# Moving the mask setup, eight gathers, a q load and the token weights' layout, and giving small attention operations to ScalarE, in a fused block-sparse attention and mixture-of-experts kernel

## The chip, the cores and the metric

The kernel runs on one core of a Trainium2 chip. The metric is the device time of one execution in microseconds (us). The core has five instruction streams that run in order and wait for one another through semaphores: TensorE (PE, whose weight loads are listed apart as PEld), VectorE (DVE), ScalarE (ACT), GpSimd (POOL) and SyncE (SP), which here only issues transfers.

## The reference

The program computes a block-sparse attention and feeds it to a small mixture of experts. There are 4 batches, 8 heads, 768 positions and 64 elements per head. Positions form 24 blocks of 32. A block of queries sees its own block and its two neighbours, the first and the last block, and three sampled blocks; the first and the last block of queries see everything.

```python
scores = scale * np.matmul(q, k.transpose(0, 1, 3, 2))
mask = np.abs(blk_i - blk_j) <= 1
mask = mask | (blk_i == 0) | (blk_j == 0) | (blk_i == n_blocks - 1) | (blk_j == n_blocks - 1)
for qb in range(n_blocks):
    for kb in sampled_blocks[qb]:
        mask[qb*32:(qb+1)*32, kb*32:(kb+1)*32] = True
attn = softmax(where(mask, scores, -1e9))      # sum + 1e-9 in the denominator
x = (attn @ v) as 3072 tokens x 512
p = domain_probs / (domain_probs.sum(-1) + 1e-9)
for e in range(4):
    out += p[:, e:e+1] * (relu(x @ w1[e]) @ w2[e])   # 512 -> 1024 -> 512
```

## The kernel before, in words

**Two kinds of attention units.** A batch has 16 units. Four are "Edge" units: for the first and the last query block, all heads at once against one half of the keys (`m` = 0 or 1); the two halves are joined afterwards with the running maximum (`mx`), the weight `w` and the sums. Twelve are "Group" units: four neighbouring query blocks `t` with four heads (`u` = 0 or 1) against 8 slots of keys. Each unit has four steps: `S` (scores into PSUM, maxima, exponentials), `T` (transposes of the probabilities through PSUM into `pt`), `A` (product with v, reciprocal of the sums, scaling into `xg`) and `X` (transpose of the result into `xr`, the expert layers' input). A Group's `S` ends in four rounds of one DVE operation (mask, add, minimum, L372) and one ACT exponential (L374). The reciprocal in `A` starts from `sums + 1e-9` (L402); for an Edge from `sums0 * w + 1e-9 + sums1` (L481, L482).

**Batch 0, the setup.** For batch 0 the units run as a software pipeline, loop L1164: in round `n` the program writes `S` of unit `n`, `X` of `n-3`, `A` of `n-2` and `T` of `n-1`. POOL and ACT copy each query block's eight key blocks into a tile `kr` (`copy_k`), SP loads the values' windows and first blocks, and the sampled value blocks come either as three loads of 64 KB from SP or, for 15 query blocks, as a gather that POOL issues (`next_gather`, L213). The first four gathers are issued in round 1; from round 2 on each round issues one, and ahead of it POOL writes one zero into the last tile `pt` (L1187). That memset has to wait until `A` has read the tile, which spaces the gathers, and the next `T` that takes the same buffer has to wait for the memset. The mask's parts (`ind`, `mask`, L279 to L284) are made on POOL after the first `copy_k`. The tile of q for group `t` comes from a pool of two, loaded in odd rounds.

**The stream.** From about 79 us on the expert products of batch 0 (`first`, `second`, with `L754` and `L827` as their matmuls) run as a generator, into which the attention of batch 1 is laced at even spacing; batches 2 and 3 are laced in the same way into `first7` and `second7` (`L754`, `L991`), a seven-product scheme. Products are grouped by 6 or 12 matmuls. Sums of several products are kept in PSUM tiles `w`, `v`, `u0`, `u1`, read by DVE (L892 to L902, L1001, L869) or ACT before PE may write on. A hidden tile gets its token's weight for the expert in L869, by the tile `pb`: one expert's weights for a batch, in all 128 partitions, read back from a scratch tensor `prt` in DRAM. `pb` lives where the raw weights lay, so the pool is opened only when the generator `spare` (`sums_w2`), which prepares combinations of w2, is used up: `more()`, L1025, advances it once per step, and twice once the first products are all written.

**Order.** Every engine runs its instructions in the order in which the program writes them. SP's transfers go round eight semaphores: the ninth waits for the first to land.

Of the kernel before, what the change touches and what calls it, by code (L numbers as in the profile page):

```python
# [8 lines left out]
F32 = mybir.dt.float32  # L9
# [8 lines left out]
P = 128  # L18
# [5 lines left out]
def attention_moe_kernel(ctx: ExitStack, tc, qb, kb, vr, sampled, sampled_t, probs, w1, w2, out):  # L24
# [5 lines left out]
    S = NT // B  # L30
    E = probs.shape[2]
    NCH, FT = w2.shape[0], w2.shape[1]
# [74 lines left out]
    def blocks(t):  # L107
        return range(1 + QG * t, min(1 + QG * (t + 1), NB - 1))

    def load_q(b, t):  # L110
        js = blocks(t)
        q = gp.tile([P, QG, P], F32, name="q")
        nc.sync.dma_start(q[:, :len(js)], qb[b, :, js[0]:js[-1] + 1])
        gathered[b, t] = q, {}, {}
# [113 lines left out]
    one = const.tile([1, 1], F32, name="one")  # L228
    nc.vector.memset(one, 1.0)
    warm = const.tile([1, 1], F32, name="warm")  # L230
    nc.scalar.activation(warm, one, AF.Exp)
# [44 lines left out]
    def mask_parts():  # L276

        ind = p1.tile([NB, NG, P], F32, name="ind")
        nc.gpsimd.memset(ind, -BIG)  # L279
        nc.gpsimd.affine_select(out=ind, in_=ind, pattern=[[P, NG], [1, P]], compare_op=ALU.is_ge,  # L280
                                fill=0.0, base=BLOCK, channel_multiplier=-BLOCK)
        nc.gpsimd.affine_select(out=ind, in_=ind, pattern=[[-P, NG], [-1, P]], compare_op=ALU.is_ge,
                                fill=0.0, base=-1, channel_multiplier=BLOCK)
        nc.gpsimd.memset(mask, 0.0)  # L284
        mk["ind"] = ind
# [47 lines left out]
    class Group:  # L333
# [53 lines left out]
        def A(self):  # L387
# [13 lines left out]
            rec = at.tile([P, 2 * HH], F32, name="rec")  # L401
            nc.vector.tensor_scalar(rec[:n], self.sums[:n], 1e-9, None, op0=ALU.add)  # L402
            nc.vector.reciprocal(rec[:n], rec[:n])
# [15 lines left out]
    class Edge:  # L419
# [5 lines left out]
        def S(self):  # L425
# [19 lines left out]
            if m == 1:  # L445
                nc.vector.tensor_max(self.mx[:, 1], self.mx[:, 0], self.mx[:, 1])
            nc.vector.tensor_scalar(nm, self.mx[:, m], -SCALE, None, op0=ALU.mult)
            if m == 1:
# [16 lines left out]
        def A(self):  # L465
# [14 lines left out]
            rec = at.tile([P, 2], F32, name="rec2")  # L480
            nc.vector.tensor_mul(rec, self.sums[:, 0], self.w)  # L481
            nc.vector.scalar_tensor_tensor(rec, rec, 1e-9, self.sums[:, 1], op0=ALU.add, op1=ALU.add)  # L482
            nc.vector.reciprocal(rec, rec)
# [335 lines left out]
    def second(b, c, g, f, j):  # L819
# [16 lines left out]
        tok = b * KT + g * (HS // P) + j  # L836
        pe = pr[:, tok, e:e + 1]
        if c == 0:
# [10 lines left out]
    def load_weights(i):  # L849
        if i < (B - 1) * E:  # L850
            b, e = 1 + i // E, i % E
            pb[b, e] = later["p"].tile([P, KT, P], F32, name="pb")
            nc.sync.dma_start(pb[b, e], bass.AP(prt.tensor, prt.offset + (b * KT * E + e) * P,
                                                [[0, P], [E * P, KT], [1, P]]))

    blk = {}

    def first7(b, c, s, n):
# [8 lines left out]
        def finish(half, g, src):  # L867
            q = pb[b, c // CPE].rearrange("p t k -> p (t k)")[:, g * HS:(g + 1) * HS]
            nc.vector.scalar_tensor_tensor(block(g, half), src, 0.0, q, op0=ALU.max, op1=ALU.mult)  # L869
# [145 lines left out]
    def experts():  # L1015
# [9 lines left out]
        def more():  # L1025

            if p > L and later.get("p") is None:
                next(spare, None)
                if p == len(one) and next(spare, None) is None:
                    only_raw.close()  # L1030
# [95 lines left out]
    def spread_weights():  # L1126

        n = NT // P * E
        t = pool["a"].tile([P, P], F32, name="prt_ps", tag="a")
        nc.tensor.transpose(t[:n], pr.rearrange("p t e -> p (t e)"), ident)  # L1130
        rows = later["t"].tile([P, P], F32, name="prows", tag="t2", bufs=2)
        nc.scalar.copy(rows[:n], t[:n])
        nc.sync.dma_start(prt, rows[:n])


    pr = const.tile([P, NT // P, E], F32, name="pr")
    psum_e = const.tile([P, NT // P], F32, name="psum_e")

    def token_weights():
        nc.vector.reduce_sum(psum_e, pr, axis=AX.X)  # L1140
        nc.vector.tensor_scalar(psum_e, psum_e, 1e-9, None, op0=ALU.add)
        nc.vector.reciprocal(psum_e, psum_e)
        nc.vector.tensor_mul(pr, pr, psum_e.unsqueeze(2).broadcast_to([P, NT // P, E]))

    with ExitStack() as only:
# [18 lines left out]
        for n in range(N + 3):  # L1164
# [6 lines left out]
            if 0 <= n - 3 < N:  # L1171
                us[n - 3].X()
            if n == 0:
                copy_k(0, 0)
            if n == 2:
                copy_k(0, 1)
            t = (n - E0) // 2
            if n > E0 and t + 2 < NG + (n % 2 == 0):
                if n % 2:
                    load_q(0, t + 2)  # L1180
                copy_k(0, t + 2 - (n % 2 == 0), (0, 1) if n % 2 else (2, 3))
            if 0 <= n - 2 < N:
                us[n - 2].A()
                if due:

# [6 lines left out]
            if n == 2:  # L1192
                place_mask()
            if n < NG - 2:
                row_blocks(n + 2)
            for t, c in rows.get(n, ()):
                load_v0(t, c)
            if n == 0:
                load_q(0, 1)
                mask_parts()  # L1200
            if n == 1:
                for _ in range(QG):
                    next_gather()
            for h in firsts.get(n, ()):
# [133 lines left out]
```

## Time and profile before

| | us |
|---|---|
| median of three runs | 1234.24 (1231.65 to 1234.75) |
| profiled execution, own time | 1232.82 |
| its span | 1231.1 |
| between span and time | 1.7 |
| PE busy | 1189.1 (97% of the span) |
| DVE, ACT, POOL busy | 808.7, 519.8, 838.4 |
| granted TensorE clock, mean | 0.993 |

The span is the profile's own stretch from first to last instruction. PE is busy for nearly all of it, so the end moves only where PE stands still or runs at a reduced clock. A row of the timeline has start, duration, engine, line, operation, tiles and count, and in brackets the idle time before it and what ended that. A row of the waits has the total, the number and the longest of them in us.

### The profile page before, as it was taken

Reading aid. Unit: us, or ns where it says so; the run is one execution under the profiler, and the core shown is the slowest. Engines: PE = TensorE matmul, PEld = TensorE weight load, DVE = VectorE, ACT = ScalarE, POOL = GpSimd, SP = SyncE. Lnnn points to the kernel's source line nnn. Section 1 sums busy time; section 2 is a strip of 40 time slices with the busy share of each in tenths; the row PEclk is TensorE's granted clock in tenths of the full one; section 3 lists DMA queues with packets and bytes.
Section 4 is the critical chain, followed back from the end, with each engine's and each line's share of the span. In section 5 each row is a group of like instructions: output and inputs, shape, how many; then the busy total and the mean of one; then the engine's idle time right before and its main releaser. Section 6 shows DMA issues by size and latency. Waiting matters only on the chain.

```text
span 1231.1 us, 32030 instructions
## 1 busy us (share of the span) xinstructions
PE 1189.1 (97%) x12243; PEld 1095.4 (89%) x12243; DVE 808.7 (66%) x1701; ACT 519.8 (42%) x1259; POOL 838.4 (68%) x824
## 2 busy tenths in 40 slices
PE   7899999999999899999999999999999999999997
PEld 4678888888888898989989999989999999999997
DVE  4774757565654667767666867766566676666667
ACT  3864555656552243444533244444533333222221
POOL 7837978888776575767647775766755776666662
PEclk8999999999999899999999999999999999999999
DMA  9986869899979787888969786989876688887874
GB/s 289 264 281 232 312 246 351 290 316 318 307 266 351 227 242 233 259 278 274 270 211 345 227 267 222 286 252 283 285 253 209 219 271 266 258 262 251 255 239 154
DMA packets 214564, 326.81 MB, mean 265 GB/s; under 512 B 17483, under 2 KB 117420, under 8 KB 214412
## 3 DMA queue, kind: packets, MB, share of 16 engines
q1 hardware_dynamic: 207888, 303.53, 76.2%
q0 software_dynamic: 6480, 21.24, 5.8%
q8 instruction: 97, 1.59, 0.6%
q14 instruction: 55, 0.45, 0.1%
q10 hardware_dynamic: 44, 0.00, 0.0%
HBM read 257.02 MB, written 67.68 MB: 264 GB/s over the span
## 4 chain that ended last, share of the span: by engine, by line
PE 79%; DVE 5%; DMA 1%; issue 1%; ACT 1%; SPq 0%; POOL 0%; DVEq 0%; ACTq 0%
PE w L754 19%; PE u L991 15%; PE v L754 14%; PE v L991 12%; PE po L827 8%; PE o L396 3%; PE tp L383 2%; PE s L362 2%; PE s L355 1%; DVE ha L869 1%; PE x L415 1%; DMA pb<-prt 1%; DMA v<-in_vr_dram 1%; PE sw L433 1%; DVE tot L1001 1%
## 5 line engine op out<-in xcount | busy, mean ns | idle before, releaser
L915 POOL TENSOR_TENSOR ho<-ha,ho 128x768 fp32r<-128x768 f32 x165 | 318.3, 1938 | 244.8 <-ACT ho L914 242.0
L754 PE MATMUL w<-xo,wo 128*128 128x384 f32 x1524 | 310.9, 340 | 10.9 <-DVE ha L869 3.5
L754 PEld LDWEIGHTS w<-xo,wo 128*128 128x128 f32 x1524 | 268.8, 189 | 19.5 <-DVE ha L902 3.9
L914 ACT CAST ho<-ha 128x768 fp32r<-128x768 f32 x168 | 139.2, 837 | 269.9 <-DVE ha L869 106.1
L754 PE MATMUL v<-xo,wo 128*128 128x384 f32 x1176 | 238.9, 339 | 1.5 <-DVE xr L417 1.0
L991 PE MATMUL u<-ho,w2o 128*128 128x384 f32 x1128 | 228.2, 338 | 2.3 <-issue 2.3
L754 PEld LDWEIGHTS v<-xo,wo 128*128 128x128 f32 x1176 | 207.7, 189 | 6.4 <-DVE xr L417 1.1
L991 PEld LDWEIGHTS u<-ho,w2o 128*128 128x128 f32 x1128 | 197.0, 188 | 4.6 <-issue 2.9
L991 PE MATMUL v<-ho,w2o 128*128 128x384 f32 x888 | 179.8, 339 | 3.2 <-issue 1.5
L991 PEld LDWEIGHTS v<-ho,w2o 128*128 128x128 f32 x888 | 154.7, 188 | 7.1 <-DVE ha L869 2.7
L1001 DVE TENSOR_TENSOR tot<-v,tot 128x384 f32<-128x384 f32 x184 | 97.9, 552 | 91.6 <-PE v L991 90.3
L1001 DVE TENSOR_TENSOR tot<-u,tot 128x384 f32<-128x384 f32 x180 | 98.8, 552 | 47.9 <-PE u L991 47.8
L827 PE MATMUL po<-w2o,hh 128*128 128x512 f32 x384 | 123.5, 403 | 1.9 <-DVE oacc L842 1.9
L374 ACT ACTIVATE p<-p,mx 128x256 f32<-128x256 f32 (+1 forms) x192 | 95.3, 498 | 50.8 <-DVE mx L372 50.6
L213 POOL DMA_INDIRECT v<-in_vr_dram,vidx x81 | 79.9, 986 | 24.4 <-issue 17.8
L644 POOL TENSOR_TENSOR wo<-r,wo 128x256 fp32r<-128x256 f32 x92 | 72.4, 793 | 32.3 <-ACT wo L643 28.5
L372 DVE CUSTOM_DVE_ANT_1 p<-s,mask 128x256 f32<-128x256 f32 (+1 forms) x192 | 69.8, 419 | 22.0 <-PE s L362 17.0
L869 DVE SCALAR_TENSOR_TENSOR ha<-ha,pb 128x384 f32<-128x384 f32 x84 | 82.5, 982 | 0.0
L827 PEld LDWEIGHTS po<-w2o,hh 128*128 128x128 f32 x384 | 69.0, 188 | 12.6 <-DVE oacc L842 2.7
L827 PE MATMUL po<-w2o,hl 128*128 128x512 f32 x192 | 75.8, 395 | 0.0
L396 PEld LDWEIGHTS o<-v,pt 128*32 128x32 f32 x2816 | 46.1, 110 | 18.5 <-issue 13.5
L396 PE MATMUL o<-v,pt 128*32 128x64 f32 x2816 | 54.6, 221 | 5.1 <-issue 3.1
(169 smaller groups left out, 1627.3 us busy)
## 6 DMA issues: line engine op xcount, KB each, us to landing
w2o<-kept SPq DMA_DIRECT2D x168, 512.0 KB
wo<-kept SPq DMA_DIRECT2D x318, 256.0 KB
kept<-wo SPq DMA_DIRECT2D x106, 256.0 KB
v<-in_vr_dram SPq DMA_DIRECT2D x88, 192.0 KB
kept<-w2o SPq DMA_DIRECT2D x32, 512.0 KB
r<-in_w_dram SPq DMA_DIRECT2D x16, 512.0 KB
r<-in_w_dram SPq DMA_DIRECT2D x32, 256.0 KB
kept<-t SPq DMA_DIRECT2D x32, 256.0 KB
```

The source lines that it names most:

```text
L213: nc.gpsimd.indirect_dma_start(out=v[:, i, 1 - i], out_offset=None, in_=vr, element_offset=b * S * DM, in_offset=bass.IndirectOffsetOnAxis ...
L372: nc.vector.tensor_tensor_reduce(p.rearrange("p (a b) -> p a b", b=BLOCK), s[h][:n, i], mk, -SCALE, 3.0e38, ALU.add, ALU.min, mx[:n])
L374: nc.scalar.activation(p, p, AF.Exp, bias=mx[:n], scale=-1.0, accum_out=self.sums[:n, m:m + 1])
L396: nc.tensor.matmul(o[cs, m], self.pt[:, 2 * m + k, cs], vs[c][:, k, e], start=k == 0, stop=k == 1)
L644: nc.gpsimd.tensor_sub(o[:, 1], src, f32(o[:, 0]))
L754: nc.tensor.matmul(ps, w[:, wi, t], x[:, xi, t], start=fresh and m == 0, stop=m == 3 * KH - 1, skip_group_check=not fresh)
L827: nc.tensor.matmul(p, a[:, js], w[:, i], start=f == 0 and n == 0, stop=f == FT - 1 and n == 2)
L869: nc.vector.scalar_tensor_tensor(block(g, half), src, 0.0, q, op0=ALU.max, op1=ALU.mult)
L914: nc.scalar.copy(o[:, 0], src)
L915: eng.tensor_sub(o[:, 1], src, f32(o[:, 0]))
L991: nc.tensor.matmul(ps, w[:, j, wi, ds], h[:, hi, j], start=fresh and m == 0, stop=m == 5, skip_group_check=not fresh)
L1001: nc.vector.tensor_add(t, ps, t)
```

## The change

Six edits are made together.

1. `mask_parts()` is called in round 0 ahead of `copy_k(0, 0)`, and `copy_k(0, 1)` in round 1 instead of 2. The tile `ind` is taken from the pool of the probabilities.
2. The first eight gathers are issued two by two in rounds 2 to 5 with no memset ahead of them; the memset and one gather per round remain from round 6 on.
3. A third tile `q2` for q: groups 2 and 5 of batch 0 use it, group 2 is loaded in round 2, and the others in even rounds from 6.
4. The host lays the token weights out by expert (`[128, expert, token tile]`), so that `prt` holds an expert's weights for a batch in one run of 768 numbers and `pb` is one run per partition, instead of six runs of 128.
5. `more()` advances `spare` one step more when the first products are all written.
6. On ACT instead of DVE: the negated maximum of an Edge (L447), `sums + 1e-9` of the Groups of batches 1 to 3 (L402), and the Edge's denominator (L481, L482: three ACT operations).

The rows of PE are the same and in the same order. On POOL, in the setup, the piece from the end of the second group's key copies (kr) to the first copy of the third group; first before, then now:

```order
L158 COPY kr_421<-k 128x128
L1187 MEMSET ptw 1x1
L213 DMA v_343<-in_vr_dram,vidx 128x512
L1187 MEMSET ptw 1x1
L213 DMA v_343<-in_vr_dram,vidx 128x512
L1187 MEMSET ptw 1x1
L213 DMA v_503<-in_vr_dram,vidx 128x512
L153 COPY kr_194<-k 128x384
```

```order
L165 COPY kr_362<-k 128x128
L220 DMA v_281<-in_vr_dram,vidx 128x512 x2
L220 DMA v_286<-in_vr_dram,vidx 128x512 x2
L220 DMA v_407<-in_vr_dram,vidx 128x512 x2
L160 COPY kr_201<-k 128x384
```

The three memsets of `ptw` are gone, and the first four gathers, which stood ahead of the second group's copies, now stand behind them.

On SP, at the end of batch 0's expert products, the stores of w2's combinations (kept), the finished outputs (oacc), and the loads of `pb`; before, then now:

```order
L725 DMA kept_7_1_1_6390<-r_6023 128x512
L692 DMA kept_7_0_1_6260<-w2o 128x1024
L672 DMA w2o<-kept_0_0_0_1291 128x4x256
L853 DMA pb<-prt 128x6x128 x2
L672 DMA w2o<-kept_0_0_1_1726 128x4x256
```

```order
L740 DMA kept_7_1_1_6390<-r_6028 128x512
L859 DMA out_dram<-oacc 128x512
L868 DMA pb<-prt 128x768 x2
L707 DMA kept_7_0_1_6265<-w2o 128x1024
L687 DMA w2o<-kept_0_0_0_1293 128x4x256
```

The two loads of `pb` now stand ahead of a store and of a load of w2 that has to wait for PE to free its tile.

On ACT, a Group's four exponentials in batch 2 and what follows, up to the next copies out of PSUM (xr, pt); before, then now:

```order
L374 ACTIVATE p,sums<-p,mx 128x256 x4
L158 ISA
L158 COPY kr_2720<-k 128x128
L417 COPY xr<-x 128x4x128
L385 COPY pt<-tp 128x512 x2
```

```order
L383 ACTIVATE p,sums<-p,mx 128x256 x4
L412 ACTIVATE rec<-sums,eps 128x4
L165 ISA
L165 COPY kr_2721<-k 128x128
L429 COPY xr<-x 128x4x128
L394 COPY pt<-tp 128x512 x2
```

The sums plus 1e-9 of the unit before (`rec`) stand behind the four exponentials of the unit after it; on DVE the reciprocal now waits for ACT there.

```diff
@@ -28,7 +28,7 @@
     S = NT // B
-    E = probs.shape[2]
+    E = probs.shape[1]
     NCH, FT = w2.shape[0], w2.shape[1]
@@ -107,9 +107,16 @@
 
+    third = []
+
     def load_q(b, t):
         js = blocks(t)
-        q = gp.tile([P, QG, P], F32, name="q")
+        if b or t not in (2, 5):
+            q = gp.tile([P, QG, P], F32, name="q")
+        else:
+            if not third:
+                third.append(p1.tile([P, QG, P], F32, name="q2"))
+            q = third[0]
         nc.sync.dma_start(q[:, :len(js)], qb[b, :, js[0]:js[-1] + 1])
@@ -227,6 +234,8 @@
     nc.vector.memset(one, 1.0)
+    eps = const.tile([P, 1], F32, name="eps")
+    nc.vector.memset(eps, 1e-9)
     warm = const.tile([1, 1], F32, name="warm")
@@ -275,7 +284,7 @@
 
-        ind = p1.tile([NB, NG, P], F32, name="ind")
+        ind = pool["p"].tile([NB, NG, P], F32, name="ind", tag="p")
         nc.gpsimd.memset(ind, -BIG)
@@ -399,7 +408,10 @@
             rec = at.tile([P, 2 * HH], F32, name="rec")
-            nc.vector.tensor_scalar(rec[:n], self.sums[:n], 1e-9, None, op0=ALU.add)
+            if b:
+                nc.scalar.activation(rec[:n], self.sums[:n], AF.Identity, bias=eps[:n])
+            else:
+                nc.vector.tensor_scalar(rec[:n], self.sums[:n], 1e-9, None, op0=ALU.add)
             nc.vector.reciprocal(rec[:n], rec[:n])
@@ -444,7 +456,7 @@
                 nc.vector.tensor_max(self.mx[:, 1], self.mx[:, 0], self.mx[:, 1])
-            nc.vector.tensor_scalar(nm, self.mx[:, m], -SCALE, None, op0=ALU.mult)
+            nc.scalar.mul(nm, self.mx[:, m], -SCALE)
             if m == 1:
@@ -478,8 +490,11 @@
             rec = at.tile([P, 2], F32, name="rec2")
-            nc.vector.tensor_mul(rec, self.sums[:, 0], self.w)
-            nc.vector.scalar_tensor_tensor(rec, rec, 1e-9, self.sums[:, 1], op0=ALU.add, op1=ALU.add)
+            last = at.tile([P, 2], F32, name="last2")
+            nc.scalar.activation(last, self.sums[:, 1], AF.Identity, bias=eps)
+            for h in range(2):
+                nc.scalar.activation(rec[:, h:h + 1], self.sums[:, 0, h:h + 1], AF.Identity,
+                                     bias=last[:, h:h + 1], scale=self.w[:, h:h + 1])
             nc.vector.reciprocal(rec, rec)
@@ -834,7 +849,7 @@
         tok = b * KT + g * (HS // P) + j
-        pe = pr[:, tok, e:e + 1]
+        pe = pr[:, e, tok:tok + 1]
         if c == 0:
@@ -849,9 +864,8 @@
             b, e = 1 + i // E, i % E
-            pb[b, e] = later["p"].tile([P, KT, P], F32, name="pb")
-            nc.sync.dma_start(pb[b, e], bass.AP(prt.tensor, prt.offset + (b * KT * E + e) * P,
-                                                [[0, P], [E * P, KT], [1, P]]))
+            pb[b, e] = later["p"].tile([P, S], F32, name="pb")
+            nc.sync.dma_start(pb[b, e], bass.AP(prt.tensor, prt.offset + e * NT + b * S, [[0, P], [1, S]]))
 
@@ -865,7 +879,7 @@
         def finish(half, g, src):
-            q = pb[b, c // CPE].rearrange("p t k -> p (t k)")[:, g * HS:(g + 1) * HS]
+            q = pb[b, c // CPE][:, g * HS:(g + 1) * HS]
             nc.vector.scalar_tensor_tensor(block(g, half), src, 0.0, q, op0=ALU.max, op1=ALU.mult)
@@ -1026,6 +1040,8 @@
                 next(spare, None)
+                if p == len(one):
+                    next(spare, None)
                 if p == len(one) and next(spare, None) is None:
@@ -1127,20 +1143,20 @@
         t = pool["a"].tile([P, P], F32, name="prt_ps", tag="a")
-        nc.tensor.transpose(t[:n], pr.rearrange("p t e -> p (t e)"), ident)
+        nc.tensor.transpose(t[:n], pr.rearrange("p e t -> p (e t)"), ident)
         rows = later["t"].tile([P, P], F32, name="prows", tag="t2", bufs=2)
...
 
-    pr = const.tile([P, NT // P, E], F32, name="pr")
+    pr = const.tile([P, E, NT // P], F32, name="pr")
     psum_e = const.tile([P, NT // P], F32, name="psum_e")
...
     def token_weights():
-        nc.vector.reduce_sum(psum_e, pr, axis=AX.X)
+        nc.vector.reduce_sum(psum_e, pr.rearrange("p e t -> p t e"), axis=AX.X)
         nc.vector.tensor_scalar(psum_e, psum_e, 1e-9, None, op0=ALU.add)
         nc.vector.reciprocal(psum_e, psum_e)
-        nc.vector.tensor_mul(pr, pr, psum_e.unsqueeze(2).broadcast_to([P, NT // P, E]))
+        nc.vector.tensor_mul(pr, pr, psum_e.unsqueeze(1).broadcast_to([P, E, NT // P]))
 
@@ -1171,17 +1187,16 @@
             if n == 0:
+                mask_parts()
                 copy_k(0, 0)
-            if n == 2:
+            if n == 1:
                 copy_k(0, 1)
...
             if n > E0 and t + 2 < NG + (n % 2 == 0):
-                if n % 2:
-                    load_q(0, t + 2)
                 copy_k(0, t + 2 - (n % 2 == 0), (0, 1) if n % 2 else (2, 3))
...
                 us[n - 2].A()
-                if due:
+                if due and n > 5:
 
@@ -1191,16 +1206,17 @@
                 place_mask()
+            if n == 2 or n > 4 and n % 2 == 0 and n // 2 < NG:
+                load_q(0, 2 if n == 2 else n // 2)
             if n < NG - 2:
...
                 load_q(0, 1)
-                mask_parts()
-            if n == 1:
-                for _ in range(QG):
-                    next_gather()
+            if n in (2, 3, 4, 5):
+                next_gather()
+                next_gather()
             for h in firsts.get(n, ()):
@@ -1320,7 +1336,7 @@
         'sampled_t': np.ascontiguousarray(sampled_blocks.T),
-        'probs': np.ascontiguousarray(moe_domain_probs.reshape(-1, P, E).transpose(1, 0, 2)),
+        'probs': np.ascontiguousarray(moe_domain_probs.reshape(-1, P, E).transpose(1, 2, 0)),
 
```

## The prediction

> **What bounds the kernel now.** I read the page's busy times and its chain first, then the windows, then the timeline of the stretches where PE (TensorE) stands still.
>
> ```profile
> PE 1189.1 (97%) x12243; PEld 1095.4 (89%) x12243; DVE 808.7 (66%) x1701; ACT 519.8 (42%) x1259; POOL 838.4 (68%) x824
> PE 79%; DVE 5%; DMA 1%; issue 1%; ACT 1%; SPq 0%; POOL 0%; DVEq 0%; ACTq 0%
> ```
> PE is the bound, and the change leaves its instructions alone. So only PE's idle time, 1231.1 - 1189.1 = 42 us, and its reduced clock can move. The windows (PE, PEld, DVE, ACT and POOL busy, then PE's granted clock, DMA share, GB/s) tell where they lie:
>
> ```profile
> 0.00:80.00 80.00, 63.87 (x1487) 43.32 (x1488) 53.59 (x212) 49.09 (x168) 57.51 (x133) 0.96 0.95 285
> 80.00:1231.00 1151.00, 1125.28 (x10758) 1052.06 (x10757) 755.09 (x1489) 470.74 (x1092) 780.90 (x691) 1.00 0.82 264
> 25.00:30.00 5.00, 2.90 (x54) 2.41 (x54) 2.40 (x11) 2.24 (x8) 4.41 (x12) 0.50 0.93 311
> ```
> The setup loses 16 us, the other 1151 us lose 26. PE's timeline around the slow window, and what the two other engines did at its start:
>
> ```profile
> 18.41 0.88 PE L474 MATMUL ow<-vn,ptw 128*32 128x64 f32 x48
> 27.10 1.51 PE L474 MATMUL ow<-vn,ptw 128*32 128x64 f32 x48 [5.10 <-ACT ptw L463]
> 28.53 1.54 PE L462 MATMUL tw<-ident,pw 128*128 128x128 f32 x6
> 16.12 1.13 POOL L213 DMA_INDIRECT v<-in_vr_dram,vidx  x1 [0.17 <-DVE ptw L463]
> 21.00 0.41 POOL L151 COPY kr<-k 128x256 f32<-128x256 f32 x1
> 26.44 0.09 POOL L1187 MEMSET ptw<- 1x1 f32 x1
> 26.56 0.48 ACT L463 COPY ptw<-tw 128x384 f32<-128x384 f32 x1 [5.06 <-POOL ptw L1187]
> ```
> At 22 us PE is stopped for 5.10 us by a copy into `ptw`, the copy by a 90 ns memset, and the memset by POOL's queue: four gathers from 16.12, then the key copies of the second group from 21.00 to 26.44. Afterwards PE's clock is down: the L474 group takes 1.51 instead of 0.88.
>
> The largest stall after that is at the start of the second expert stage:
>
> ```profile
> 392.04 0.32 SPq L725 DMA_DIRECT2D kept<-r  x1
> 393.61 1.95 SPq L853 DMA_DIRECT2D pb<-prt  x2
> 393.61 7.41 DMA pb<-prt
> 401.12 0.56 DVE L869 SCALAR_TENSOR_TENSOR ha<-v,pb 128x384 f32<-128x384 f32 x1 [6.32 <-DMA pb<-prt]
> 395.55 2.28 PE L754 MATMUL w<-xo,wo 128*128 128x384 f32 x12
> 397.67 2.28 PE L754 MATMUL v<-xo,wo 128*128 128x384 f32 x12
> 403.16 4.18 PE L754 MATMUL w<-xo,wo 128*128 128x384 f32 x12 [3.20 <-DVE ha L869]
> 407.13 3.24 PE L754 MATMUL v<-xo,wo 128*128 128x384 f32 x12
> 410.21 2.24 PE L754 MATMUL w<-xo,wo 128*128 128x384 f32 x12
> ```
> `pb` is issued at 393.61 and lands 7.41 later (the chain's row), and DVE's L869 waits 6.32 for it. Groups of twelve start 397.67 - 395.55 = 2.12 apart. The group at 410.21 would start at 397.67 + 3 x 2.12 = 404.03: it is 6.2 us late, 3.4 of it in the first step and 1.9 and 1.0 in the next two, in which DVE works off what it is behind. (The rows are two of SP, one of the chain of waits, one of DVE and five of PE.)
>
> **The change part by part.** The sum is made against the profiled 1232.82; the median of the runs stands 1.4 above it.
>
> *Memsets, gathers, mask (edits 1, 2).* No memset stands ahead of the first eight gathers, so ACT's copy waits for PE's transposes alone and PE goes on at about 22.0. I expect the stall of 5.10 to go and the slow clock behind it in part: (1.51 - 0.88) + (1.54 - 0.87) is about 1.3. What is late next: the join of the first Edge unit. Its denominator is now three ACT operations behind four exponentials:
>
> ```profile
> 32.92 0.16 DVE L481 TENSOR_TENSOR rec<-edge,ew 128x2 f32<-128x2 f32 x1
> 33.49 0.49 ACT L374 ACTIVATE p<-p,mx 128x256 f32<-128x256 f32 x1
> L454 ACT ACTIVATE ew<-ew 128x2 f32<-128x2 f32 x8 | 1.6, 198 | 0.0
> ```
> In the join quoted DVE could start at 32.92, while ACT's last exponential ends at about 34.0. Three operations of 0.2 (L454 is the nearest in shape) put the reciprocal at 34.6 instead of some 33.3 (two operations of 0.19 behind 32.92): 1.3 late. PE's transpose of the result comes right behind, so I charge 1.4. The mask's 3 us on POOL move into POOL's first wait for the keys and cost nothing there; without that cover, 3.
>
> How far the gain lasts depends on the rows of values and on q:
>
> ```profile
> 44.73 0.39 SPq L113 DMA_DIRECT2D q<-in_qb_dram  x1
> 49.78 1.10 PE L352 MATMUL s<-kr,q 64*32 64x256 f32 x32 [1.43 <-DMA q<-in_qb_dram]
> SPq L184 <- DMA r<-in_w_dram: 1.7, 2, 1.1
> ```
> q is issued at 44.73 and PE waits 1.43 for it. Issued one or two rounds earlier (edit 3) it is there in time, so 1.4 is won. Against this, SP's transfers go round eight semaphores, and DMA is at 0.95 of its time in this stage: the three loads of values per block (L184) wait for landings, not for PE, and come only 2 to 3 us earlier. Above, the work is 5.1 + 1.3 - 1.4 + 1.4 = 6.4; the transfers let 2 to 5 through. I take **-3.8**; bounds 0 (the transfers set the end of the setup) and -6.4.
>
> *`pb` (edits 4, 5).* The loads move ahead of `kept<-w2o` and of `w2o<-kept`, but stay behind the store of 392.04; the issue comes at about 392.5, 1.1 earlier. For the landing (runs of 3 KB instead of 512 B) the trace has no like. The nearest is the q above, 256 KB, which took 5.05 from its issue to PE's start; the gathers of values, 192 KB, lie around it:
>
> ```profile
> DMA to landing us min/median/max: 3.6/5.8/8.4
> ```
> With 5.1 (an estimate from q) it lands at 397.6. L869 is needed twice before PE writes `w` again at 397.67 + 2.12 = 399.8; two of 0.56 fit. So the 6.2 go. If it still takes 7.41, it lands at 399.9, PE waits some 1.2 + 0.8, and 4.2 is won. POOL makes the products' third `xo` about 2.5 us later than before, just as PE asks for it: +0.3. Sum **-5.9**, bounds -4.2 and -6.2. The operations of edit 4 on DVE are the same in number and size. With `spare` used up a step earlier, L644 and L672 move by one product, in POOL's and SP's slack.
>
> *Attention on ACT (edit 6).* 68 operations leave DVE and 71 reach ACT, which is busy for 42%:
>
> ```profile
> L402 DVE TENSOR_SCALAR rec<-sums 128x4 f32<-128x4 f32 (+1 forms) x48 | 21.5, 448 | 0.0
> L402 DVE TENSOR_SCALAR rec<-sums x48: 152/220/1773, 36.3 to 937.0; 128x4 f32<-128x4 f32 x40, 64x4 f32<-64x4 f32 x8
> 544.69 0.90 DVE L402 TENSOR_SCALAR rec<-sums 128x4 f32<-128x4 f32 x1
> 545.73 0.19 ACT L374 ACTIVATION_READ_ACCUMULATOR p<-p,mx 128x1 f32 x1
> 546.24 0.55 DVE L902 TENSOR_TENSOR ha<-w,ha 128x384 f32<-128x384 f32 x1
> 546.85 1.31 PE L754 MATMUL w<-xo,wo 128*128 128x384 f32 x6 [1.61 <-DVE ha L902]
> 585.14 0.50 ACT L374 ACTIVATE p<-p,mx 128x256 f32<-128x256 f32 x1
> 585.89 0.56 DVE L902 TENSOR_TENSOR ha<-w,ha 128x384 f32<-128x384 f32 x1
> 586.73 1.21 PE L754 MATMUL w<-xo,wo 128*128 128x384 f32 x6
> ```
> L402 takes 152 ns where nothing holds it, and up to 1773; on ACT it costs some 0.2, but behind the exponentials. At 544.69 it ran until 545.59. Now ACT's exponentials end at 545.92 and the sum at 546.12: the reciprocal, and behind it L902 and PE's wait of 1.61, come 0.5 later. At 585 the delay is larger: the last exponential ends at about 585.7, the sum at 585.9, reciprocal and scaling at about 586.6, where L902 now starts instead of 585.89. It ended 0.28 before PE's row; so PE waits 0.45. Two more groups, near 623 and 801 us, have a reader as close: four places, 2.0. Of the 36 moved sums most have no reader that PE waits for within a microsecond; for these I add 1.0. Against it, where DVE was held in an Edge join, ACT is quicker:
>
> ```profile
> 491.09 1.67 DVE L481 TENSOR_TENSOR rec<-edge,ew 128x2 f32<-128x2 f32 x1
> 492.79 1.76 DVE L482 SCALAR_TENSOR_TENSOR rec<-rec,edge 128x2 f32<-128x2 f32 x1
> PE w L754 <- DVE ha L892: 1.3, 1, 1.3
> ```
> These two last 3.4 us and L892, behind them, lets PE wait 1.3: gone, with 0.7 at another `xe` (751 us). Sum 2.0 + 1.0 - 2.0 = **+1.0**; bounds -3 and +7 (12 more places of 0.5).
>
> The Trainium skill, "ScalarE: Activation LUTs", "Rules for kernel authors", tells authors to put add and mul on VectorE, not ScalarE. By its row alone each moved operation would lose 198 - 152 = 46 ns here, 71 x 0.046 = 3.3 us if all were in PE's way; the mean of 448 ns on DVE speaks against that.
>
> **Sum.** -3.8 - 5.9 + 1.0 = -8.7: 1224.1 for an execution like the profiled one, with 1.4 for the median about **1225.5 us**.
>
> **The rivals.**
> *B: the transfers hold the setup.* For it speak the DMA share of 0.95 and SP's waits for landings; against it, that PE's 5.10 are not a wait for DMA. The first term is 0: 1229.3.
> *C: DVE waits for ScalarE, and PE for DVE.* The place is L403, which now stands behind ACT's four exponentials. The price is 0.9 (1.2 of delay less 0.28 of slack), and it decides if nearly all of the 24 Groups of batches 2 and 3 pay it: 21.6 instead of 1.0, 1246, slower than before. Half of them, 11 us: 1235.5, no change. For it speaks the slack of 0.28 at 585; against it, that PE's waits for DVE behind 80 us are few, and that many L902 start only when PE is done.
> *D: `pb` still late*, since stores are queued ahead: a stall of 4 remains, 1229.5.
> *E: DVE gains more than it waits.* DVE loses 21.5 - 48 x 0.152 = 14 us of being held in L402 alone, three quarters of it moved away; of PE's waits for L902, L892 and their neighbours 3 go where I have 1.0 coming, and the setup keeps 5.1: 1232.82 - 5.1 - 5.9 - 3 + 1.4 = 1220.2. The Trainium skill, "SBUF — State Buffer", "SBUF: two separate sides", calls the port pair of VectorE and GpSimd an exclusive lock, which ScalarE never waits on; L402's 152 to 1773 against 198 throughout for L454's group agrees, and favours E.
>
> **How the numbers follow.** Forecast 0.50; B 0.15; C 0.15, of which 0.07 slower and 0.08 no change; D 0.08; E 0.12. A difference of 0.3%, 3.7 us, is about what a measurement can tell. Faster, below 1230.5: all of the forecast but 0.03, B and D but 0.05 together, E: 0.77. Same: 0.16. Slower: 0.07. The forecast's bounds, taken as independent (root of the sum of squares: 4.8 down from 2.6, 0.3 and 4; 7.3 up from 3.8, 1.7 and 6), give 1220.7 to 1232.8. The range 1219.5 to 1233 takes in most of E too and leaves out 0.05 below and 0.15 above.
>
> **What would show it.** Right: no wait for a memset at 22 us and the first 80 us of the profile shorter by 4; PE's group behind 397.67 on time, L869 without a wait for `pb`; PE's waits for L902 at 545 and 802 of about 2.1. Wrong: new waits of PE for L404's or L902's outputs at many groups (C), q or values as releasers between 25 and 70 us (B), a wait for `pb` above 2 us (D).

## The result, and the profile after

The changed kernel takes **1247.21 us** (median of five runs, 1246.42 to 1248.20) where the kernel before takes 1234.24: a ratio of 1.0106, with a 95% interval of 1.0086 to 1.0125. It is slower by 13 us. The forecast was 1225.5 with a range of 1219.5 to 1233, so sign and size were wrong; the time lies next to the 1246 of rival C at its full price.

The page of the changed kernel, and its windows in the columns used before:

```profile
PE 1197.4 (96%) x12243; PEld 1099.1 (88%) x12243; DVE 785.8 (63%) x1634; ACT 536.2 (43%) x1335; POOL 839.5 (67%) x820
0.00:80.00 80.00, 64.97 (x1408) 42.28 (x1408) 47.87 (x192) 49.70 (x174) 55.37 (x127) 0.89 0.87 264
80.00:1245.00 1165.00, 1132.44 (x10836) 1056.82 (x10835) 737.90 (x1442) 486.48 (x1162) 784.18 (x693) 1.00 0.81 262
```
PE's idle time grew from 42 to 48 us and its busy time from 1189.1 to 1197.4: the same 12243 matmuls took 8.3 us longer. Most of that goes with the reduced clock: its mean was 0.988 instead of 0.993, which is some 6 us of the span (an estimate from these two means). DVE did 23 us less work, as the change meant it to. So DVE became emptier and PE waited for it more. The waits of DVE and of PE behind the setup (total, number, longest) show why:

```profile
DVE rec L415 <- ACT rec L412: 41.8, 29, 2.9
DVE rec L498 <- ACT rec L496: 12.8, 5, 3.5
PE w L769 <- DVE z L828: 4.9, 4, 3.6
PE w L769 <- DVE ha L916: 2.7, 3, 2.1
PE w L769 <- DVE xg L416: 2.1, 1, 2.1
PE v L769 <- DMA wo<-kept: 1.5, 1, 1.5
```
L412 is the moved sum (L402 before), L415 the reciprocal, L496 and L498 the same of an Edge, L916 was L902 and L828 was L813. In the kernel before, DVE waits for no `rec` at all. Now it stands still for 41.8 us in 29 Groups and 12.8 us in 5 Edge joins.

PE runs the same matmuls in the same order in every kernel of this study. So the start of the n-th matmul can be compared between two profiles, and its lateness tells in which stretch time was lost. The table gives what each stretch added, in us against the profile of the kernel before; a stretch is named by the time of the kernel before at which it ends. The setup is the first two columns (the stream starts there), the Edge join of batch 1 lies in the third, `pb` in the fifth, the Groups of batches 2 and 3 in the sixth. Each row is one profiled execution.

| kernel | 38 us | 93 | 169 | 394 | 427 | 954 | end | span |
|---|---|---|---|---|---|---|---|---|
| changed | +3.7 | +2.0 | +3.7 | +1.3 | -5.5 | +8.6 | +0.4 | +14.3 |
| changed, once more (e8) | -1.1 | +0.8 | +4.8 | +1.6 | -5.4 | +7.8 | +1.8 | +10.2 |
| e1: edits 1 to 3 | -5.5 | +5.4 | 0.0 | -1.2 | -1.7 | +0.2 | +1.4 | -1.4 |
| e4: no memset | -5.5 | +8.1 | 0.0 | -0.5 | -0.5 | -0.4 | 0.0 | +1.2 |
| e9: 1.5 MB more | +1.8 | +5.7 | -0.1 | -0.9 | +0.7 | -0.2 | 0.0 | +6.9 |
| e2: edits 4, 5 | -0.3 | +1.7 | 0.0 | -0.1 | -5.4 | +0.9 | +0.1 | -3.2 |
| e7: edits 1 to 5 | -5.1 | +4.4 | 0.0 | +0.4 | -5.6 | +0.6 | 0.0 | -5.3 |
| e3: edit 6 | +2.2 | +1.6 | +3.8 | +0.7 | -0.6 | +7.3 | +0.7 | +15.7 |
| e5: edit 6, Groups | -0.5 | +3.7 | -0.1 | +1.1 | +0.4 | +7.9 | +1.7 | +14.2 |
| e10: edit 6, Edges | +1.5 | +1.8 | +4.8 | -2.0 | -1.0 | +1.5 | +0.4 | +6.9 |
| e6: edit 6, early | +0.6 | +0.8 | -1.3 | -1.4 | -0.4 | -2.9 | +0.4 | -4.2 |
| e11: all, early | -0.8 | +2.0 | -1.3 | +0.4 | -4.9 | -3.8 | +0.4 | -8.0 |
| e12: e11, late w2 | -1.9 | +2.2 | -1.3 | +0.1 | -5.0 | -4.3 | +0.4 | -9.9 |

Two profiles of one kernel differ by a few us in the setup (first two columns: +5.7 and -0.3 for the changed kernel), and by about one elsewhere. The setup's columns are therefore read only where several kernels agree.

**The Groups.** The place at 545 us of the kernel before, in the changed one (ACT, DVE, DVE, DVE, PE), and a window of four us that begins just behind PE's restart (columns as above, PE's clock third from the end); then the window behind the same place in the kernel before, and the Group near 801 us in the changed kernel, PE and window:

```profile
552.09 0.28 ACT L412 ACTIVATE rec<-sums,eps 128x4 f32<-128x4 f32 x1
552.40 0.18 DVE L415 RECIPROCAL rec<-rec 128x4 f32<-128x4 f32 x1 [1.36 <-ACT rec L412]
552.68 0.42 DVE L416 TENSOR_TENSOR xg<-o,rec 128x256 f32<-128x256 f32 x1
553.02 0.55 DVE L916 TENSOR_TENSOR ha<-w,ha 128x384 f32<-128x384 f32 x1
553.62 1.82 PE L769 MATMUL w<-xo,wo 128*128 128x384 f32 x6 [2.12 <-DVE xg L416]
554.00:558.00 4.00, 4.00 (x16) 4.00 (x15) 2.08 (x5) 0.00 (x0) 0.69 (x1) 0.57 0.81 245
547.00:551.00 4.00, 4.00 (x27) 3.97 (x28) 2.31 (x5) 0.73 (x2) 1.11 (x2) 1.00 0.97 275
814.85 1.33 PE L769 MATMUL w<-xo,wo 128*128 128x384 f32 x6 [2.10 <-DVE ha L916]
814.00:818.00 4.00, 3.15 (x18) 3.15 (x19) 3.31 (x7) 0.00 (x0) 1.62 (x2) 1.00 1.04 272
```
The wait is 2.12 where it was 1.61: the 0.5 that the prediction worked out. What it left out is the clock. PE's mean clock in these 4 us is 0.57; at 0.5 that is some 3.4 us of half speed, in which 1.7 us of work are lost. With the wait of 1.61 in the kernel before, the clock stayed at 1.00. The slow stretch follows this place in all four profiles whose Groups have the sums on ACT behind the next unit (changed, e8, e3, e5; waits of 2.04 to 2.12) and in no other. The length of the wait does not decide it alone, though: near 801 us the same four profiles have waits of 2.06 to 2.11, and there the clock stays at 1.00 and PE loses the forecast's 0.5. What else decides stays open. The table's sixth column holds this place with +2.1 of its +8.6.

**The Edge join at 157 us.** DVE, PE, and the clock behind, in the changed kernel; the last row is PE at this place in the kernel before:

```profile
162.27 0.17 DVE L498 RECIPROCAL rec<-rec 128x2 f32<-128x2 f32 x1 [2.42 <-ACT rec L496]
164.75 2.03 PE L769 MATMUL w<-xo,wo 128*128 128x384 f32 x6 [3.60 <-DVE z L828]
165.00:169.00 4.00, 4.00 (x17) 3.60 (x17) 1.11 (x2) 2.31 (x7) 2.78 (x3) 0.57 0.76 236
156.77 1.31 PE L754 MATMUL w<-xo,wo 128*128 128x384 f32 x6 [1.33 <-DVE z L813]
```
DVE waits 2.42 for the third of ACT's operations, and the hidden layer's L828 stands behind the join on DVE. PE's wait grows from 1.33 to 3.60, and again the clock goes down: +3.7 in all.

**`pb`.** SP, the chain of waits, PE twice:

```profile
403.07 1.32 SPq L868 DMA_DIRECT2D pb<-prt  x2
403.07 5.99 DMA pb<-prt
411.19 2.32 PE L769 MATMUL w<-xo,wo 128*128 128x384 f32 x12 [0.59 <-DVE ha L883]
420.19 0.97 PE L769 MATMUL v<-xo,wo 128*128 128x384 f32 x4 [1.48 <-DMA wo<-kept]
```
The load lands 5.99 after its issue (7.41 before); PE waits 0.59 instead of 3.20, and the groups behind are on time. A new wait of 1.48 for a load of `wo` comes 9 us later.

**The setup.** PE three times (a wait, then the first and the last of six short gaps), and the clock:

```profile
14.40 1.11 PE L486 MATMUL ow<-vn,ptw 128*32 128x64 f32 x48 [2.36 <-ACT ptw L475]
23.08 0.43 PE L486 MATMUL ow<-vn,ptw 128*32 128x64 f32 x3 [0.19 <-issue]
27.37 0.46 PE L486 MATMUL ow<-vn,ptw 128*32 128x64 f32 x5 [1.11 <-issue]
15.00:23.00 8.00, 7.15 (x86) 5.11 (x77) 2.15 (x7) 1.20 (x5) 6.92 (x17) 0.50 0.76 212
23.00:28.00 5.00, 2.48 (x18) 1.24 (x19) 1.18 (x5) 2.38 (x9) 2.71 (x3) 0.50 0.97 313
```
No wait for a memset is left at 22 us. But PE now waits 2.36 at 12 us, as ACT copies the second group's keys ahead of `ptw`; the clock stands at 0.50 from 15 to 28 us; and between 23 and 28 us PE gets its matmuls a few at a time, with no releaser in the profile.

### The profile page after: what moved, and what is told of

Same layout as the page of the kernel before. It is cut to its first block, busy times and chain, and to the rows that moved or that the text cites. A ratio compares the mean times of both kernels' runs of the same rounds, so it can differ in the third digit from the quotient of the medians.

```text
span 1245.4 us, 31994 instructions
## 1 busy us (share of the span) xinstructions
PE 1197.4 (96%) x12243; PEld 1099.1 (88%) x12243; DVE 785.8 (63%) x1634; ACT 536.2 (43%) x1335; POOL 839.5 (67%) x820
## 4 chain that ended last, share of the span: by engine, by line
PE 79%; DVE 7%; DMA 5%; ACT 4%; issue 3%; POOL 1%; SPq 1%; ACTq 0%; DVEq 0%; POOLq 0%
PE w L769 19%; PE u L1005 15%; PE v L769 14%; PE v L1005 11%; PE po L842 7%; PE o L405 3%; PE tp L392 3%; ACT p L383 2%; PE s L371 1%; DMA wo<-kept 1%; PE s L364 1%; DVE ha L883 1%; DVE hl L788 1%; PE ow L486 1%; DVE tot L1015 1%
```

## The experiments

Theory 1 after the result: the parts add up; the ACT part loses 12 us or more, `pb` wins 5, the setup wins nothing or loses. The rivals are that the ACT moves are even and the setup alone is at fault, or that the parts disturb one another.

**e1: edits 1 to 3 alone.**

```diff
             if n == 0:
+                mask_parts()
                 copy_k(0, 0)
-            if n == 2:
+            if n == 1:
                 copy_k(0, 1)
...
-                if due:
+                if due and n > 5:
...
+            if n in (2, 3, 4, 5):
+                next_gather()
+                next_gather()
...
```


> Edits 1 to 3 alone (mask first, the second group's keys one round earlier, eight gathers unbound, third q tile); attention's small operations stay on VectorE and the weights' layout is as before. Theory 1 (the setup's loss is these edits' own): PE reaches its first L754 group 5 to 6 us later than in the kernel before, the clock is at 0.5 from about 15 to 32 us, and the time is 5 to 7 us longer. Rival (ScalarE's moved operations in the Edge units make PE wait at 12 us and so start the slow clock): PE waits less than 1.5 us at 12 to 14 us, the clock stays at 1.0 until 20 us, and the time is 0 to 4 us shorter, as the prediction had it.

Measured: 1234.12, ratio 1.0003 (0.9980 to 1.0025). Neither theory is right. PE is 5.5 us ahead at 38 us (the prediction had 6.4 of work won) and has lost all of it when the stream starts. PE's wait of 2.2 for ACT's copy into `ptw` is there without edit 6, and the clock still stays at 1.00 up to 50 us, so the slow clock of the changed kernel was not these edits' doing alone. The waits of PE up to 82 us that were not in the kernel before name transfers of values, 5.1 us in all; those with releaser "issue" are 3.0, about as before (3.1):

```profile
PE o L403 <- DMA v<-in_vr_dram: 3.8, 3, 1.5
PE ow L481 <- ACT ptw L470: 2.4, 2, 2.2
PE s L359 <- issue: 1.7, 2, 1.5
PE o L403 <- issue: 1.3, 2, 1.1
PE o L403 <- DMA v<-in_vr_dram,vidx: 1.3, 1, 1.3
```

**e2: edits 4 and 5 alone.**

```diff
-            pb[b, e] = later["p"].tile([P, KT, P], F32, name="pb")
+            pb[b, e] = later["p"].tile([P, S], F32, name="pb")
...
                 next(spare, None)
+                if p == len(one):
+                    next(spare, None)
```


> Edits 4 and 5 alone (token weights by expert, one step more of spare). Theory: the stall behind pb goes and nothing else moves: 5 to 7 us shorter, about 1228. Rival (the load of wo that PE waits 1.5 us for in the changed kernel at 413 us comes with these edits): 4.5 us shorter and that wait is there.

Measured: 1230.28, ratio 0.9976 (0.9962 to 0.9990), 3 us shorter. The stretch of `pb` wins 5.4 in its profile, near the forecast's amount and the theory's. The medians show 3, with an interval of 1 to 5, less than the theory's 5 to 7. The rival's sign is there: PE waits 1.00 for a load of `wo` at 410 us, as it does (0.9 to 1.5) in every profile with these edits and not in the kernel before. The setup, which these edits don't touch, was 1.4 us later in this profile: that is the size of its scatter.

**e3: edit 6 alone.**

```diff
-            nc.vector.tensor_scalar(rec[:n], self.sums[:n], 1e-9, None, op0=ALU.add)
+            if b:
+                nc.scalar.activation(rec[:n], self.sums[:n], AF.Identity, bias=eps[:n])
+            else:
+                nc.vector.tensor_scalar(rec[:n], self.sums[:n], 1e-9, None, op0=ALU.add)
...
-            nc.vector.tensor_scalar(nm, self.mx[:, m], -SCALE, None, op0=ALU.mult)
+            nc.scalar.mul(nm, self.mx[:, m], -SCALE)
...
+            nc.scalar.activation(last, self.sums[:, 1], AF.Identity, bias=eps)
...
```


> Edit 6 alone (negated maxima, sums plus 1e-9 and the Edge denominators on ScalarE). Theory 1 (VectorE waits for ScalarE at the join of an Edge unit and at the Groups whose reader follows closely): PE waits 3 to 4 us near 156 us for z, 0.5 to 1 us at 545, 585, 625, 665 and 801 us, in all 9 to 12 us longer, about 1244. Rival (setup edits only; these moves are even): within 3 us of the kernel before.

Measured: 1247.30, ratio 1.0100 (1.0070 to 1.0129). Theory 1 holds: this edit alone has the whole loss, and the rival falls.

**e4: the memset alone is left out in rounds 2 to 5.**

```diff
                     u = us[n - 2]
-                    nc.gpsimd.memset(u.pt[:1, u.end - 1:, u.n - 1:u.n], 0.0)
+                    if n > 5:
+                        nc.gpsimd.memset(u.pt[:1, u.end - 1:, u.n - 1:u.n], 0.0)
                     next_gather()
```


> One line of edit 2 alone: the memset is left out in rounds 2 to 5, the gathers stay at their places in the program, mask, keys and q as before. Theory (the memset behind POOL's queue was the whole stall of 5.1 us, and PE is not held by anything else until 30 us): PE goes on at about 22 us and the time is 4 to 6 us shorter. Rival (the transfers or PE's instruction supply hold the setup): the 5 us come back as waits before 80 us, and the time is within 2 us of before.

Measured: 1234.13, ratio 1.0006 (0.9993 to 1.0020). The rival was right. The stall of 5.1 is gone (5.5 ahead at 38 us) and comes back in four pieces and more, of PE:

```profile
38.33 1.92 PE L352 MATMUL s<-kr,q 64*32 64x256 f32 x32 [2.43 <-DMA q<-in_qb_dram]
47.24 0.59 PE L352 MATMUL s<-kr,q 64*32 64x256 f32 x2 [2.38 <-issue]
57.04 0.63 PE L396 MATMUL o<-v,pt 128*32 128x64 f32 x26 [1.44 <-issue]
64.45 0.32 PE L396 MATMUL o<-v,pt 128*32 128x64 f32 x8 [2.47 <-issue]
```
Counting PE's matmuls, weight loads and sequencer rows in the trace, the three stalls with releaser "issue" stand at numbers 1473, 1986 and 2242: 513 and 256 apart. Each of the 14 profiles has such a stall at one or more places of this row, multiples of 256 apart (give or take one). The page's row of the instruction queue (q8) fits that (packets, MB, share of the transfers' time):

```profile
q8 instruction: 97, 1.59, 0.6%
```
These are 16 KB a packet, and 97 packets for 24486 matmuls and weight loads are 252 a packet. In the trace of e4, packets of this queue end at 45.66, 55.60 and 62.95 us, and PE goes on 1.4 to 1.6 us later each time. PE is waiting for its own program.

The Trainium skill, "Runtime: NRT & Kernel Launch", "Instruction fetch mechanics", says that an engine's instructions are refilled in blocks of 256 by DMA while the current block runs, and that a crossing is mostly hidden. The spacing agrees with these rows; hidden it is not here, where a crossing costs up to 2.47 us.

**e5: of edit 6 the Groups' sums only**, the first piece of the diff of e3.

> Of edit 6 only the Groups' sums plus 1e-9 of batches 1 to 3 (36 operations) go to ScalarE; the Edge units stay on VectorE. Theory (every moved sum makes VectorE wait for the next unit's exponentials, and the Edge joins are a separate cost of some 7 us at 27, 37 and 157 us): 5 to 7 us longer, about 1239, PE loses nothing before 200 us, and 0.5 to 1 us each near 545, 585, 625 and 801 us. Rival (the whole loss is the Edge joins'): within 2 us of before.

Measured: 1247.00, ratio 1.0097 (1.0066 to 1.0127): 12 us, twice what the theory gave. The stream of its profile is 11.0 us longer (the last five columns), with +2.1 at 545 us, 1.1 at 585, 0.9 at 625 and about 0.5 each near 800, 830, 860 and 900; at most of DVE's other waits PE's start shows no such step. Some 3 us of its setup's lateness touch nothing that the edit changed (batch 0 stays on DVE) and are scatter. DVE's wait is the one that names the cause:

```profile
DVE rec L408 <- ACT rec L405: 48.7, 34, 2.9
```

**e6: the same operations on ACT, but written directly behind the unit's own exponentials.**

```diff
                     nc.scalar.activation(p, p, AF.Exp, bias=mx[:n], scale=-1.0,
                                          accum_out=self.sums[:n, m:m + 1])
+            if b:
+                nc.scalar.activation(self.sums[:n], self.sums[:n], AF.Identity, bias=eps[:n])
...
-            nc.vector.tensor_scalar(rec[:n], self.sums[:n], 1e-9, None, op0=ALU.add)
-            nc.vector.reciprocal(rec[:n], rec[:n])
+            if b:
+                nc.vector.reciprocal(rec[:n], self.sums[:n])
...
```
The Edge's denominator is made at the end of its S step in the same way.

> Edit 6 with the same operations on ScalarE, but written one place earlier: directly behind the unit's own exponentials (the sums of a Group in place, the Edge's denominator at the end of its S step), so that VectorE's reciprocal, two rounds later, finds them done. Theory 1 (the loss is the place, behind the next unit's exponentials, and not the engine): the 13 us are gone, 0 to 4 us shorter than before, about 1232, and PE has no wait for z above 1.5 us at 157 us. Rival (ScalarE is too slow or too full for them, wherever they stand): 8 us longer or more.

Measured: 1229.72, ratio 0.9969 (0.9951 to 0.9986). Theory 1 holds: the same operations on the same engine, 16 us apart from e3. The place in ACT's queue is the loss, not the engine. DVE has no wait for ACT's `rec`; at the place of 545 us PE waits 0.66 where it waited 1.61 in the kernel before and 2.12 in the changed one:

```profile
541.55 0.17 DVE L407 RECIPROCAL rec<-sums 128x4 f32<-128x4 f32 x1
542.77 1.33 PE L764 MATMUL w<-xo,wo 128*128 128x384 f32 x6 [0.66 <-DVE ha L912]
```

**e7: the changed kernel without edit 6**, the edits of e1 and e2 together.

> The changed kernel without edit 6: edits 1 to 5. Theory (parts add up: setup 0, pb -3 to -5): about 1229, and the halting supply of PE at 23 to 28 us, seen in the changed kernel, is not there. Rival (edits 1 to 5 disturb one another, and the setup's loss of 5.8 us in the changed kernel is not edit 6's): 1233 or more, PE's first L754 group 3 us or more later than before.

Measured: 1229.08, ratio 0.9948 (0.9932 to 0.9965). The theory's 1229 is met, and PE has no short gaps at 23 us. The ratios of e1 and e2 multiply to 0.9979, so the parts add up only at the edge of what the intervals allow. Its setup wins 5.1 and gives 4.4 back.

**e8: the changed kernel once more.** No edit.

> The changed kernel once more, one look. If the six short gaps of PE between 23 and 28 us, for which the profile shows no releaser, belong to the kernel, they are there again and PE's first L754 group starts at 84 to 87 us; if they were an accident of that execution, they are gone and it starts at 82 to 84 us.

Measured: 1242.99 in one execution. The short gaps and the long slow clock are gone, and the setup ends 0.3 us earlier than that of the kernel before. They belonged to that execution, or to its chip; what made them stays open. The stream of this profile, 10.5 us longer, carries the loss by itself.

**e9: a transfer more.** The kernel before, with 1.5 MB that nothing reads.

```diff
+            if n == 4:
+                extra = dram.tile([S, DM], F32, name="extra")
+                nc.scalar.dma_start(extra, vr[:S])
```


> The kernel before with one transfer more: 1.5 MB from DRAM to DRAM, issued by ScalarE in round 4 of the setup (some 30 us), which nothing waits for. Theory (between 30 and 80 us the setup goes at the pace of its transfers, 285 GB/s at 0.95 of their time, so that what PE gains at 22 us is given back): 3 to 5 us longer, as 1.5 MB over 285 GB/s is 5.5 us and some 0.05 of the time is free; the waits are PE's for its instructions at 256 apart, for q and for values. Rival (the setup goes at the pace of its chain of work, and transfers have room): within 1.5 us of before.

Measured: 1239.71, ratio 1.0048 (1.0032 to 1.0064), 5.9 us longer (4 to 8 by the interval). That is a little more than the theory's 3 to 5, and the rival falls. PE's waits up to 86 us:

```profile
PE o L396 <- issue: 5.5, 3, 2.2
PE s L352 <- DMA q<-in_qb_dram: 1.2, 1, 1.2
```
No wait for the extra transfer exists. The kernel before had, up to 79 us:

```profile
PE o L396 <- issue: 3.1, 4, 1.8
```
Its wait for q was 1.6 in all, so that one did not grow. The waits with releaser "issue" are 2.4 us longer here, but these reach 5.1 in e11 and 7.6 in e4 with no transfer more. Where PE pays for the 1.5 MB is therefore not settled by this profile; that it pays is.

**e10: of edit 6 the Edges' part only**, the second and third piece of the diff of e3.

> Of edit 6 only the Edge units' part (negated maxima, denominators: 16 and 24 operations on ScalarE); the Groups stay on VectorE. Theory (parts add up: the table of PE's starts gives the Edge joins 3.8 us at 157 us and 1 to 2 more, the Groups 9): 4 to 6 us longer, about 1238. Rival (the Groups' 36 operations are the whole loss, since they alone measured as much as all of edit 6): within 2 us of before.

Measured: 1239.51, ratio 1.0057 (1.0036 to 1.0077), 6 to 7 us longer, at or just above the upper end of the theory's 4 to 6, and the rival falls. DVE and PE at the join of batch 1:

```profile
159.81 0.17 DVE L488 RECIPROCAL rec<-rec 128x2 f32<-128x2 f32 x1 [2.42 <-ACT rec L486]
162.30 2.29 PE L759 MATMUL w<-xo,wo 128*128 128x384 f32 x6 [3.62 <-DVE z L818]
```
The Groups alone (12) and the Edges alone (6 to 7) make more than edit 6 (12). Their streams are 11.0, 3.6 and 11.9 us longer: some three us are not accounted for, which the intervals allow.

**e11 and e12: all six edits, edit 6 early; and, in e12, three loads of raw w2 later** (both of round 4 and that of round 8).

```diff
-        seconds = {3: 3, 4: 2, 6: 1, 8: 1}
+        seconds = {3: 3, 6: 1, 15: 1, 16: 1, 17: 1}
```


> All six edits, with edit 6 written early (directly behind the unit's own exponentials). Theory (gains of the parts add up, 0.9948 and 0.9969): 0.992 of before, about 1223 to 1226, faster than both kernels. Rival (early sums only pay where VectorE is late, and the setup takes back what it gains): 1228 to 1230.

> As e11, and three of the seven loads of raw w2 in the setup (256 KB each) are issued in rounds 15 to 17 instead of 4, 6 and 8. Theory (transfers set the pace of the setup between 30 and 70 us): PE's first L754 group starts 1 to 2.5 us earlier than in e11 and the time is 1 to 2.5 us shorter. Rival (instructions' latency alone sets it, 5 us for 256 instructions at any load): no difference from e11 above 0.5 us.

Measured: e11 1226.21, ratio 0.9940 (0.9921 to 0.9960); e12 1223.51, ratio 0.9933 (0.9911 to 0.9954). Both are faster than both kernels. For e11 the sum of the parts, 0.9917, lies just below the interval; the rival's 1228 lies above the median, and neither is refuted cleanly. What e12 adds is not told apart from e11: its setup was 0.9 us shorter and the intervals overlap.

## Why the prediction was wrong

**The setup, -3.8: rival B was right.** The stall of 5.1 did go, and most of the slow clock behind it (e1, e4, e7: 5.1 to 5.5 ahead at 38 us). The step that failed is "the transfers let 2 to 5 through". They let nothing through: 1.0003 and 1.0006. That the transfers bound the setup from 30 to 80 us is what e9 supports: 1.5 MB more cost 5.9 us, where the 285 GB/s of the first window give 5.5. A run with fewer bytes in the setup, the other way round, was not made (e12 only moves them). The quoted DMA share of 0.95 stood in the argument for B; the forecast read it as a limit for the row loads alone and let these come 2 to 3 us earlier. In e1 the waits for values took back 5.1 us; in e4 the gain went to waits for PE's own program (7.6 us against 3.1 in the kernel before) and for q (3.3 against 1.6). PE's own program was missing from the working.

**`pb`, -5.9: right.** The stretch won 5.4 to 5.6 in four of the six profiles with edits 4 and 5 (4.9 and 5.0 in e11 and e12), with 0.59 left of the wait and 1.48 of a new one for `wo`. The estimate of 5.1 for the landing was low (5.99), and the wait for `wo` was not in the working. The wait for `xo` was 0.29, as taken. The runs of e2 alone show less, 1 to 5.

**Attention on ACT, +1.0: the term that decided, and the step that failed.** It measured +12 (e3; 9 to 16 by the interval). In its steps:
- The four places were the right ones, the delays too (2.12 was forecast as 1.61 + 0.5). PE's wait at the fourth was 2.10, as forecast too. The price was right there only: +2.1, +1.1, +0.9 and +0.6 (e5) instead of 0.5 each, and the first was followed by 3.4 us of half clock.
- "For these I add 1.0", for all other Groups: 29 of 36 reciprocals wait for L412, 41.8 us of DVE in all, and DVE carries those delays into its next operations. The stream of e5 lost 11.0, of which the four places have 4.7.
- The Edge joins were credited with -2.0 and cost 6 to 7 (e10). The credit at 496 us did come where the denominator was early (e6); behind the exponentials of the next unit, the join at 157 us alone cost 3.7 to 4.8. The prediction costed such a join in the setup at 1.4 and not in the stream.
- 76 operations reached ACT (1259 to 1335), not 71; the forecast's sum did not use that count.
- "On ACT it costs some 0.2": L412 measured 280 to 300 ns, not the 198 of L454. L412 has its bias in a tile of one number per partition, L454 has not. Of the Edge's three operations the first has such a bias (279 to 292), and the other two have bias and scale in tiles (372 to 391). The forecast took 0.2 for each. The Trainium skill, "ScalarE: Activation LUTs", "What ACT_TABLE_LOAD costs", gives 280 ns and 0.833 per element for that form, and the runs agree. The Trainium skill's rule on add and mul ("Rules for kernel authors" of the same page, as in the prediction) has the sign of the changed kernel but not that of e6, where the same operations on ScalarE made the kernel 4 us faster: here the place decided, and not the engine's speed.

**The rivals.** C described what happened, at about half its price: DVE waits 1.4 us on the mean in 29 of 36 Groups, PE pays about 0.3 per Group on the mean (11.0 over 36, the slow clock included), and the Edges come on top. It had 0.15, of which 0.07 for slower. E's mechanism exists as well: freed of the small operations and not waiting for them, DVE lets PE go on 5.6 us earlier in the stream of e6 (the last five columns). It needed the early place.

With the measured terms the sum is 0 - 5.5 + 12 = +6.5 in place of -8.7; the changed kernel measured +13 in one set of runs and +8.4 in the single run of e8 against 1234.64. By the table the difference of the two lies in the setup, and it is open. The ratios of e7 and e3 multiply to 1.0047, below the interval of the first set, so it is not excluded that edits 1 to 5 and edit 6 disturb one another there.

## What to carry to other kernels

An operation that moves to another engine takes a place in that engine's queue: write it directly behind what makes its input, not where its reader stands, or the first engine waits for whatever the second does in between. When a wait of the bounding engine grows, look at the clock behind it as well: one wait of 2.1 us here cost 2.1 us more, another of the same length 0.5. Where transfers are busy for 0.95 of a stage, as in this setup, expect a stall removed there to be given back; whether fewer bytes in the stage would have kept the gain was not tested.

## What the runs showed of the hardware

- Most of PE's longer stalls without a releaser lie 256 instructions, or a multiple of it, apart, one 16 KB packet of the instruction queue. In the setup the longest cost 2.9 us (e3). Their sum up to 86 us was 3.1 in the kernel before and 2.9 to 8.0 in the others; that it grows with the other transfers is not shown.
- A wait of 2.12 us was followed by 3.4 us at half speed, one of 1.61 was not; but waits of 2.10 (changed kernel, 815 us) and 2.23 (e1, 14 us) also left the clock at 1.00. The length of one wait does not tell whether the clock goes down.
- On two numbers per partition an activation took 0.20 us without a tile as operand (L459) and 0.29 with its bias in a tile (L494); with bias and scale in tiles, on one number, it took 0.38 (L496).
